# Loading parts of wo and W2 as two and six runs in an interleaved attention and MLP decode kernel

## The chip, the cores and the metric

The kernel runs on one core of one Trainium2 chip. A core has five engines that run their own instruction streams: TensorE (PE, with its weight loads PEld), VectorE (DVE), ScalarE (ACT), GpSimd (POOL) and SyncE (SP). Sixteen DMA engines move data between HBM and SBUF, the core's memory, which has 128 partitions (rows). Transfers are issued here by SP and by ACT, each with a queue of its own (q1 and q10 in the profile). The metric is device time in microseconds (us), the median over runs.

## The reference

One token passes four blocks: attention with a cached K and V, an MLP, and both again with the same weights and caches.

```python
def _A_ref(x, k_cache, v_cache, wq, wo):          # B=1, Sq=1, D=640, H=32, Sk=8192, Dh=128
    q = (x @ wq).reshape(B, Sq, H, Dh).transpose(0, 2, 1, 3)
    scores = jnp.einsum("bhqd,bhkd->bhqk", q, k_cache) * (Dh ** -0.5)
    p = _softmax(scores, axis=-1)
    o = jnp.einsum("bhqk,bhkd->bhqd", p, v_cache)
    return o.transpose(0, 2, 1, 3).reshape(B, Sq, H * Dh) @ wo

def _B_ref(x, w1, w2):                            # w1 [640, 1728], w2 [1728, 640]
    h = jnp.einsum("bsd,df->bsf", x, w1)
    return jnp.einsum("bsf,fd->bsd", jnp.maximum(h, 0), w2)

x = A_x
x = x + _A_ref(_layernorm(x), K, V, wq, wo)
x = x + _B_ref(_layernorm(x), w1, w2)
x = x + _A_ref(_layernorm(x), K, V, wq, wo)
x = x + _B_ref(_layernorm(x), w1, w2)
```

All data are float32. K and V together are 268 MB and are read twice, but for a few pieces that are kept.

## The kernel before

**Two layers.** `attention_and_mlp(L, ...)` runs for L = 0 (called layer 1 here) over heads 0 to 31 and for L = 1 (layer 2) over heads 31 to 0. Each head has a K unit and a V unit of 4 MB (128 partitions by 8,192 floats), loaded whole or, for a few heads, in pieces.

**The ring.** Units live in one SBUF tile, `ring`. `pump()` issues loads on SP's queue in a fixed order, and each as soon as a free place is found; in the bulk of layer 1 the ring has room for three whole units. `release()` frees a piece after TensorE's last use of it and calls `pump()`. So the load that takes the place of head 6's V unit is issued when the last V piece of head 6 has been multiplied.

**One head.** `scores` (line 433) multiplies the four pieces of K, VectorE takes the maximum (445, 451), ScalarE the exponentials (459), VectorE transposes them (466), `values` (484) multiplies the four pieces of V, and `output` (501 to 525) collects the result. All streams are in order: what stands behind a waiting instruction on its engine waits too.

**Side work.** Between the pieces, `side_work()` takes steps from two lists, `chores` and `slow`. `slow` holds the next group's queries and, at fixed heads, the preparation of the last head's projection. For that, `due()` at the fifth head after the first of layer 1 (`WC_AT[0] = 5`) issues on ACT's queue a load of one block of wo, 128 rows of 2,560 B, into the tile `mix` (line 676). One head later the generator `mixing()` joins `slow`: VectorE sums the rows (543) and subtracts the mean (544), TensorE transposes the block (550, 556), ScalarE copies it out (552, 564). Later `mixing_quarter()` multiplies it with W1 (571). Layer 2 does the same at head position 8.

**The MLP.** `mlp()` multiplies the hidden row with W2's 14 blocks (`times_rows`, line 402, called in `product`). Blocks 0 to 7 are in `w2_t`. In layer 2 blocks 8 to 13 go into a free place of the ring (`w2_rest`): `pump()` issues them last, by `W2_MORE` as blocks 8 and 9, 10 and 11, 12, and 13 (line 173). Block 13 has 64 rows (`W2_LAST`), the others 128. Their products are the last of the kernel, and behind them stand one VectorE instruction (858) and the output's transfer (901).

**Layout.** `_laid_out` (line 922) puts the inputs on the host into the order in which they are loaded; it does no arithmetic.

Of the kernel before, what the change touches and what calls it, by code (L numbers as in the profile page):

```python
# [15 lines left out]
P = 128  # L16
D = 640
H = 32
SK = 8192
DH = 128  # L20
# [3 lines left out]
HG = 4  # L24
NG = H // HG
# [41 lines left out]
def wide(kind, piece):  # L67

    return 4 * piece[2] * (1 if kind == "k" else DH) // 8


def size(unit):
    return sum(wide(unit[0], piece) for piece in unit[1])
# [6 lines left out]
FB = 4 * F_TILES + F_REST  # L80
SLOTS = 8
W2_PARTS = [(0, 4), (4, SLOTS)]
W2_MORE = [(SLOTS, 10), (10, 12), (12, 13), (13, FB)]
W2_LAST = 2 * (F_ROWS[2] - P * F_TILES)


@with_exitstack
def decode_kernel(ctx: ExitStack, tc: tile.TileContext, x, kv, wq, wo, w1, w2, out):
    nc = tc.nc
    consts = ctx.enter_context(tc.tile_pool(name="consts", bufs=1))  # L90
    wts = ctx.enter_context(tc.tile_pool(name="wts", bufs=1))
# [25 lines left out]
    w2_rest = []  # L117
# [8 lines left out]
    def place(layer, u, n):  # L126


        step = 8 if u in KEPT else max(m for m in (8, 64, 256, 512) if n % m == 0)
        low, high = 0, RING if layer else FLAT  # L130
        if layer == 0 and u in kept and (u in KEPT or u[0] == 30 and UNITS[30][u[1]][0] == "k"):
            low, high = (EDGE, RING) if u in KEPT else (FLAT, EDGE)
        at, best = low, None
        for a, m in sorted(live.values()) + [(high, 0)]:
            a = min(a, high)
            if a - at >= n and (best is None or a - at < best[1]):
                best = at, a - at
            at = max(at, -(-(a + m) // step) * step)
        return None if best is None else best[0]

    def pump():
        while todo:
            layer, u = todo[0]
            kind, pieces = unit = UNITS[u[0]][u[1]]
            n = size(unit)
            at = place(layer, u, n)
            if at is None:
                return
            todo.pop(0)
            o = dram_at[u]  # L150
            nc.sync.dma_start(
                ring[:, 8 * at : 8 * (at + n)],
                kv[o : o + 8 * P * n].rearrange("(p m) -> p m", p=P),
            )
            for t, piece in enumerate(pieces):
                m = wide(kind, piece)
                live[layer, u, t] = at, m
                at_of[layer, u, t] = ring, 8 * at
                at += m
            if not todo or layer < todo[0][0]:  # L160
                for a, b in W2_PARTS[:: 1 - 2 * layer]:
                    nc.sync.dma_start(w2_t[:, a:b], w2[:, a:b])
        n = (FB - SLOTS) * D // 8
        if not w2_rest:
            at = place(1, None, n)
            if at is not None:
                w2_rest.append(ring[:, 8 * at : 8 * (at + n)].rearrange("p (b d) -> p b d", d=D))
                for a, b in W2_MORE:
                    more_of_w2(a, b, w2_rest[0][:, a - SLOTS : b - SLOTS])

    def more_of_w2(a, b, where):
        rows = W2_LAST if a == FB - 1 else P
        nc.sync.dma_start(where[:rows], w2[:rows, a:b])
# [68 lines left out]
    mix = consts.tile([P, DFF], F32, name="mix")  # L242
# [55 lines left out]
    def spread_of_columns(xc):  # L298
        sq = work.tile([P, NB], F32, name="ln_sq")
        ss = work.tile([P, 1], F32, name="ln_ss")  # L300
        nc.vector.scalar_tensor_tensor(
            sq, xc, 1.0, xc, op0=ALU.mult, op1=ALU.mult, accum_out=ss
        )
        pv = bank_tile()[:, :1]
        nc.tensor.matmul(pv, ss.to_broadcast([P, P]), ones, start=True, stop=True)
        return inv_std(pv)
# [286 lines left out]
    def attention_and_mlp(L, xr, s, before=None):  # L593

        heads = list(range(H))[:: 1 - 2 * L]
        last = heads[-1]
# [60 lines left out]
        def due(h):  # L657

            where = heads.index(h)
            k, j = divmod(where, HG)  # L660
            if j == 0:
                o_cols[k] = work.tile([P, HG], F32, name="o_cols", bufs=2)
            if where and j == 0:
                chores.append([run_out(k - 1), "pe"])
            if j == 2 and k + 1 < NG:
                slow.append([queries_of(k + 1), "pe"])
            if where == H - 2:
                chores.append([first_of_last(), "pe"])
            if where == H - 1:
                chores.append([before_last(), "pe"])  # L670
            if L == 0 and where == H - HG:
                slow.append([centre_query(NG - 1, HG - 1), "pe"])
            if L == 0 and where == 4:
                nc.scalar.dma_start(w1_t, w1)
            if where == WC_AT[L]:
                nc.scalar.dma_start(mix[:, :D], wo[last // HG][:, last % HG])
            if where == WC_AT[L] + 1:
                slow.append([mixing(), "dve"])
            if where in MIX_AT[L]:
                slow.append([mixing_quarter(MIX_AT[L].index(where)), "pe"])  # L680
# [28 lines left out]
        for where, h in enumerate(heads):  # L709
# [21 lines left out]
            if h == last:  # L731
                o = work.tile([P, 1], F32, name="c_ol")
                rest = output(hd, o)
# [15 lines left out]
            else:  # L749
                k, j = divmod(where, HG)  # L750
# [8 lines left out]
    def mlp(L, o, last, xp, ph):  # L759
# [162 lines left out]
def _laid_out(A_x, A_k_cache, A_v_cache, A_wq, A_wo, B_w1, B_w2):  # L922
    k = np.asarray(A_k_cache)[0].reshape(H, 4, 4, RUN, DH).transpose(0, 4, 1, 2, 3)
    v = np.asarray(A_v_cache)[0].reshape(H, 4, 4, NBL, 4, 32, DH).transpose(0, 1, 5, 3, 4, 2, 6)
    v = v.reshape(H, P, NBL, 4, 4, DH)
    kv = np.empty(H * P * SK * 2, k.dtype)
    o = 0
    for h in range(H):
        for kind, pieces in UNITS[h]:
            n = 8 * sum(wide(kind, piece) for piece in pieces)  # L930
            block = kv[o : o + P * n].reshape(P, n)
            o += P * n
            a = 0
            for piece in pieces:
                if kind == "k":
                    r, c, m = piece
                    part = k[h, :, :, r, c : c + m]
                else:
                    b, r, m = piece
                    part = v[h, :, b, :, r : r + m]  # L940
                part = part.reshape(P, -1)
                block[:, a : a + part.shape[1]] = part
                a += part.shape[1]
    w2 = np.zeros((P, FB, D), np.asarray(B_w2).dtype)
    for b, f in enumerate(_hidden_rows()):
        w2[f >= 0, b] = np.asarray(B_w2)[f[f >= 0]][:, _COLS]

    wq = np.asarray(A_wq).reshape(NB, P, NG, HG * DH).transpose(2, 1, 0, 3)
    return {
        "x": np.repeat(np.asarray(A_x).reshape(D)[_COLS].reshape(4, DR), 32, axis=0),  # L950
        "kv": kv,
        "wq": wq.reshape(NG * P, NB * HG * DH),
        "wo": np.asarray(A_wo)[:, _COLS].reshape(NG, HG, DH, D).transpose(0, 2, 1, 3),
        "w1": np.asarray(B_w1).reshape(NB, P, DFF).transpose(1, 0, 2),
        "w2": w2,
    }


# [22 lines left out]
```

## Time and profile before

| | us |
|---|---|
| median of 3 runs | 1353.76 (1351.77 to 1354.28) |
| the profiled execution | 1351.81 |
| its span, first to last instruction | 1349.9 |
| PE, DVE, ACT busy in it | 909.9, 297.2, 58.5 |

The page tells the bulk; the windows tell how busy the 16 DMA engines are in a stretch (the share in the last but one column, where 1.00 is all sixteen); the timeline tells one instruction's start, its duration and, in brackets, the idle time of its engine before it and what ended that. A DMA's landing is told as the time from its issue until the data are there.

```profile
q1 hardware_dynamic: 24936, 530.95, 91.9%
q10 hardware_dynamic: 4608, 41.86, 7.4%
```

These are SP's and ACT's queues: packets, MB, and the share of the sixteen engines' span that they took.

### The profile page before, as it was taken

The numbers are of one execution on the slowest core, as the hardware profiler recorded it, in microseconds if no ns is written. First come the engines' busy times: TensorE is split into PE (matmuls) and PEld (weight loads), VectorE is DVE, ScalarE is ACT, GpSimd is POOL, SyncE is SP. The second block draws the span as 40 slices with busy tenths as digits, with TensorE's granted clock in tenths as the row PEclk, the third lists the DMA queues.
The fourth block names the chain that finished last, engine by engine and source line by source line (L and its number), as shares of the span: only waits on it lengthen the run. The fifth ranks groups of instructions, "written<-read, shape, count | busy, mean of one in ns | idle before, by whom it ended". The sixth has DMA issues, their size and how long they took to land.

```text
span 1349.9 us, 14049 instructions
## 1 busy us (share of the span) xinstructions
PE 909.9 (67%) x6078; PEld 282.3 (21%) x6078; DVE 297.2 (22%) x979; ACT 58.5 (4%) x147; POOL 2.9 (0%) x10
## 2 busy tenths in 40 slices
PE   5564676766667666666688776677566767668667
PEld 2111121211112112112143211222112221122113
DVE  2121121222112222122223222221121212212212
ACT  0000000000000000000000000000000000000000
POOL 0000000000000000000000000000000000000000
PEclk8676788788777777777998876778778787787889
DMA  9999999999999999999999999999999999999997
GB/s 396 435 429 430 431 429 432 432 429 432 431 429 429 430 432 430 433 425 421 428 373 426 435 430 430 429 431 431 429 432 432 425 436 428 429 434 428 432 425 325
DMA packets 29605, 573.71 MB, mean 425 GB/s; under 512 B 3300, under 2 KB 3432, under 8 KB 6376
## 3 DMA queue, kind: packets, MB, share of 16 engines
q1 hardware_dynamic: 24936, 530.95, 91.9%
q10 hardware_dynamic: 4608, 41.86, 7.4%
q8 instruction: 48, 0.79, 0.2%
q14 instruction: 13, 0.11, 0.0%
HBM read 572.80 MB, written 0.00 MB: 424 GB/s over the span
## 4 chain that ended last, share of the span: by engine, by line
DMA 70%; PE 26%; DVE 2%; issue 1%; ACT 1%; SPq 0%; ACTq 0%; DVEq 0%
DMA ring<-in_kv 69%; PE outs L484 9%; PE ps L433 9%; PE px L571 2%; PE px L360 2%; DMA ring<-in_w 1%; PE acc L402 1%; PE pm L471 1%; PE px L374 1%; ACT p L459 0%; DVE h_t L445 0%; PE pm L450 0%; PE px L402 0%; DVE p L505 0%; DVE p L466 0%
## 5 line engine op out<-in xcount | busy, mean ns | idle before, releaser
L484 PE MATMUL outs<-ring,p 128*4 128x512 f32 (+2 forms) x2160 | 347.7, 773 | 162.4 <-DMA ring<-in_kv 109.7
L433 PE MATMUL ps<-ring,spread_q 128*32 128x512 f32 (+2 forms) x2056 | 334.0, 746 | 122.6 <-DMA ring<-in_kv 121.9
L445 DVE TENSOR_REDUCE h_t<-ps 128x1 f32<-128x512 f32 x64 | 44.3, 691 | 389.4 <-PE ps L433 389.3
L433 PEld LDWEIGHTS ps<-ring,spread_q 128*32 128x32 f32 x2056 | 71.6, 130 | 261.0 <-issue 229.1
L484 PEld LDWEIGHTS outs<-ring,p 128*4 128x4 f32 x2160 | 51.4, 96 | 325.5 <-issue 162.6
L459 ACT ACTIVATE p<-ps,h_t 128x512 f32<-128x512 f32 x63 | 43.3, 687 | 1179.0 <-DVE h_t L451 1179.0
L466 DVE STREAM_TRANSPOSE p<-p 128x128 f32<-128x128 f32 x256 | 79.8, 312 | 63.6 <-ACT p L459 56.9
L518 PE MATMUL pm<-ones,p 128*128 128x1 f32 (+1 forms) x128 | 24.7, 263 | 97.6 <-DVE p L505 97.6
L501 DVE TENSOR_SCALAR p<-outs,ind 128x128 f32<-128x128 f32 x64 | 22.5, 351 | 251.5 <-PE outs L484 251.5
L505 DVE SCALAR_TENSOR_TENSOR p<-outs,ind,p 128x128 f32<-128x128 f32 x188 | 66.0, 351 | 6.7
L450 PE MATMUL pm<-ident,h_t 128*128 128x128 f32 x128 | 31.2, 325 | 40.5 <-DVE h_t L445 40.4
L518 PEld LDWEIGHTS pm<-ones,p 128*128 128x128 f32 x128 | 19.2, 190 | 161.1 <-DVE p L505 160.3
L471 PEld LDWEIGHTS pm<-ind,h_t 128*128 128x128 f32 x128 | 27.4, 266 | 82.6 <-issue 82.6
L372 DVE TENSOR_SCALAR q_row<-px,ln_r 128x128 f32<-128x128 f32 x56 | 19.5, 349 | 109.1 <-PE ps L433 71.4
L571 PE MATMUL px<-w_t,wct 128*128 128x448 f32 (+1 forms) x80 | 43.4, 627 | 0.0
L360 PE MATMUL px<-wq_t,ln_xc 128*32 128x512 f32 x140 | 41.4, 921 | 0.0
L474 DVE RECIPROCAL h_t<-pm 128x1 f32<-128x1 f32 x64 | 10.7, 168 | 119.4 <-PE pm L471 119.4
L450 PEld LDWEIGHTS pm<-ident,h_t 128*128 128x128 f32 x128 | 19.0, 187 | 85.5 <-DVE h_t L445 83.8
L471 PE MATMUL pm<-ind,h_t 128*128 128x1 f32 x128 | 32.9, 326 | 0.0
L402 PE MATMUL acc<-wo_t,o_cols 128*32 128x160 f32 x496 | 31.1, 408 | 0.0
L402 PEld LDWEIGHTS acc<-wo_t,o_cols 128*32 128x32 f32 x496 | 24.3, 151 | 17.6 <-issue 14.2
L374 PEld LDWEIGHTS px<-sel,q_row 128*128 128x128 f32 x112 | 19.9, 221 | 35.1 <-DVE q_row L372 35.1
(126 smaller groups left out, 227.3 us busy)
## 6 DMA issues: line engine op xcount, KB each, us to landing
ring<-in_kv SPq DMA_DIRECT2D x104, 4096.0 KB, 28.8
ring<-in_kv SPq DMA_DIRECT2D x29, 2048.0 KB, 27.9
wq_t<-in_wq ACTq DMA_DIRECT2D x14, 1280.0 KB, 16.7
wo_t<-in_wo ACTq DMA_DIRECT2D x14, 1280.0 KB, 17.2
ring<-in_kv SPq DMA_DIRECT2D x9, 1024.0 KB, 14.9
w_t<-in_w SPq DMA_DIRECT2D x4, 1280.0 KB, 26.8
w_t<-in_w ACTq DMA_DIRECT2D x1, 4320.0 KB, 24.4
ring<-in_kv SPq DMA_DIRECT2D x5, 768.0 KB, 19.4
```

The lines of the kernel that those rows point to most:

```text
L360: nc.tensor.matmul(pq[32 * strip : 32 * strip + 32], xc[:, c : c + 1].to_broadcast([P, 32]), wq_t[g][:, c], start=c < 4, stop=c in (1, 2, ...
L402: nc.tensor.matmul(acc[32 * g : 32 * g + 32, :DR], col.to_broadcast([col.shape[0], 32]), wt[:, g * DR : (g + 1) * DR], start=first, stop=last,
L433: nc.tensor.matmul(hd.ps[32 * g : 32 * g + 32, c : c + n], spread_q[:, 3 - r : 35 - r], tile_of[:, at + g * n : at + (g + 1) * n], start=f ...
L445: nc.vector.tensor_reduce(hd.nm, hd.ps, AX.X, ALU.max, negate=True)
L450: nc.tensor.matmul(pt[:, :P], hd.nm.to_broadcast([P, P]), ident, start=True, stop=True)
L459: nc.scalar.activation(hd.p, hd.ps, AF.Exp, bias=hd.low, scale=scale, accum_out=hd.l)
L466: nc.vector.transpose(hd.all_p[:, b * P : (b + 1) * P], hd.p[:, b * P : (b + 1) * P])
L471: nc.tensor.matmul(pt[:, :1], hd.l.to_broadcast([P, P]), ind[:, 4:5], start=True, stop=True)
L484: nc.tensor.matmul((hd.out if r0 < 2 else hd.out_2)[32 * g : 32 * g + 4, r0:r1].rearrange("p r d -> p (r d)"), hd.all_p[:, 32 * i : 32 * i ...
L505: nc.vector.scalar_tensor_tensor(oc, hd.out[:, r], ind[:, r : r + 1], oc, op0=ALU.mult, op1=ALU.add)
L518: nc.tensor.matmul(pt[:, :n], part, mask.to_broadcast([P, n]), start=i == 0, stop=i == len(parts) - 1,)
L571: nc.tensor.matmul(pt[:, :n], wct[:, c], w1_t[:, c, f : f + n], start=(c == 0), stop=(c == NB - 1),)
```

## The change

A new input `apart` holds copies of three pieces of weights, each cut into runs of whole rows with a gap of 128 floats (`GAP`) after each run. A load from it has the shape runs x rows x 640 on the side of HBM, and rows x 640 in SBUF; the gap keeps the runs from being one.

- Layer 1, wo's block into `mix`: rows 80 to 127 are loaded from `wo` as before, rows 0 to 79 from `apart` as two runs of 40.
- Layer 2, W2's block 12: rows 0 to 79 from `w2`, rows 80 to 127 from `apart` as six runs of 8.
- Layer 2, W2's block 13: its 64 rows from `apart` as two runs of 32.

Layer 1's loads of W2 and layer 2's load of wo stay. What is computed stays too.

```diff
+GAP = 128
+FEW = {"wo": (0, 80, 2), "w2": (80, P, 6), "w2_last": (0, W2_LAST, 2)}
+def few_size(name):
+    r0, r1, k = FEW[name]
+    return (r1 - r0) * D + k * GAP
...
-                for a, b in W2_MORE:
-                    more_of_w2(a, b, w2_rest[0][:, a - SLOTS : b - SLOTS])
+                rest = w2_rest[0]
+                for a, b in W2_MORE[:2]:
+                    more_of_w2(a, b, rest[:, a - SLOTS : b - SLOTS])
+                whole = FEW["w2"][0]
+                nc.sync.dma_start(rest[:whole, FB - SLOTS - 2], w2[:whole, FB - 2])
+                by_few_engines(nc.sync, "w2", rest[:, FB - SLOTS - 2])
+                by_few_engines(nc.sync, "w2_last", rest[:, FB - SLOTS - 1])
+
+    def by_few_engines(queue, name, where):
+
+        r0, r1, k = FEW[name]
+        at, n = FEW_AT[name], few_size(name)
+        part = apart[at : at + n].rearrange("(k m) -> k m", k=k)
+        queue.dma_start(
+            where[r0:r1], part[:, : n // k - GAP].rearrange("k (r d) -> k r d", d=D)
+        )
...
             if where == WC_AT[L]:
-                nc.scalar.dma_start(mix[:, :D], wo[last // HG][:, last % HG])
+                whole = 0 if L else FEW["wo"][1]
+                nc.scalar.dma_start(mix[whole:, :D], wo[last // HG][whole:, last % HG])
+                if L == 0:
+                    by_few_engines(nc.scalar, "wo", mix[:, :D])
```

In `_laid_out` the pieces are copied into `apart`. The order of the instructions on TensorE and VectorE is the same; two DMA queues have one issue more each. On ACT's queue in layer 1, around heads 4 to 6, it stood before as (line, operation, destination and source, shape):

```order
L213 DMA wo_t<-in_wo 128x2560
L459 ACTIVATE p,h_t<-ps,h_t 128x512
L676 DMA mix<-in_wo 128x640
L459 ACTIVATE p,h_t<-ps,h_t 128x512 x2
L209 DMA wq_t<-in_wq 128x2560
L552 COPY wct<-px 128x512
```

and now, with the changed kernel's line numbers:

```order
L237 DMA wo_t<-in_wo 128x2560
L483 ACTIVATE p,h_t<-ps,h_t 128x512
L701 DMA mix<-in_wo 48x640
L191 DMA mix<-in_apart 80x1x640
L483 ACTIVATE p,h_t<-ps,h_t 128x512 x2
L233 DMA wq_t<-in_wq 128x2560
L576 COPY wct<-px 128x512
```

One load became two in the same place. On SP's queue at the end of the program it stood before as:

```order
L162 DMA w_t<-in_w 128x2560 x2
L173 DMA ring<-in_w 128x1280 x2
L173 DMA ring<-in_w 128x640
L173 DMA ring<-in_w 64x640
L901 DMA out<-xr 4x160
```

and now:

```order
L172 DMA w_t<-in_w 128x2560 x2
L197 DMA ring<-in_w 128x1280 x2
L182 DMA ring<-in_w 80x640
L191 DMA ring<-in_apart 48x1x640
L191 DMA ring<-in_apart 64x1x640
L928 DMA out<-xr 4x160
```

Two loads became three. The instructions that read `mix` first stand on TensorE, in head 6 of layer 1, as they stood before (changed kernel's lines; 574 is the transposing of the block, 508 `values`):

```order
L508 MATMUL outs_113<-ring,p 4x512 x4
L495 MATMUL pm<-ind,h_t 128x1
L398 MATMUL px<-sel,q_row 128x1
L508 MATMUL outs_113<-ring,p 4x512 x8
L574 MATMUL px<-ident,mix 128x128 x4
L508 MATMUL outs_113<-ring,p 4x512 x4
```

Nothing moved here: the block's transposes stand between the third and the fourth piece of head 6's V.

More of the change, by code (lines that the diff above doesn't have):

```diff
@@ L84, with decode_kernel @@
 W2_LAST = 2 * (F_ROWS[2] - P * F_TILES)
+GAP = 128
[3 more added lines that the diff above has]
+    return (r1 - r0) * D + k * GAP
+FEW_AT = {name: sum(few_size(n) for n in list(FEW)[:i]) for i, name in enumerate(FEW)}
 @with_exitstack
-def decode_kernel(ctx: ExitStack, tc: tile.TileContext, x, kv, wq, wo, w1, w2, out):
+def decode_kernel(ctx: ExitStack, tc: tile.TileContext, x, kv, wq, wo, w1, w2, apart, out):
     nc = tc.nc
@@ L946, in _laid_out @@
         w2[f >= 0, b] = np.asarray(B_w2)[f[f >= 0]][:, _COLS]
+    wo = np.asarray(A_wo)[:, _COLS].reshape(NG, HG, DH, D).transpose(0, 2, 1, 3)
+    apart = np.zeros(sum(few_size(name) for name in FEW), w2.dtype)
+    for name, block in (("wo", wo[-1][:, -1]), ("w2", w2[:, FB - 2]), ("w2_last", w2[:, FB - 1])):
+        (r0, r1, m), at, n = FEW[name], FEW_AT[name], few_size(name)
+        part = apart[at : at + n].reshape(m, -1)
+        part[:, : n // m - GAP] = block[r0:r1].reshape(m, -1)
     wq = np.asarray(A_wq).reshape(NB, P, NG, HG * DH).transpose(2, 1, 0, 3)
@@ L952, in _laid_out @@
         "wq": wq.reshape(NG * P, NB * HG * DH),
-        "wo": np.asarray(A_wo)[:, _COLS].reshape(NG, HG, DH, D).transpose(0, 2, 1, 3),
+        "wo": wo,
         "w1": np.asarray(B_w1).reshape(NB, P, DFF).transpose(1, 0, 2),
         "w2": w2,
+        "apart": apart,
     }
```

## The prediction

> **What bounds the kernel now.** I read the page first: the slices, the queues, the chain of waits.
>
> ```profile
> DMA  9999999999999999999999999999999999999997
> DMA packets 29605, 573.71 MB, mean 425 GB/s; under 512 B 3300, under 2 KB 3432, under 8 KB 6376
> q8 instruction: 48, 0.79, 0.2%
> DMA 70%; PE 26%; DVE 2%; issue 1%; ACT 1%; SPq 0%; ACTq 0%; DVEq 0%
> ```
>
> The transfers bound it: the 16 DMA engines are busy in every slice but the last, and 70% of the chain is waiting for them. 425 GB/s over 16 engines is 26.6 GB/s each, so one row of 2,560 B occupies an engine for 0.1 us, one row of a whole ring load (32,768 B) for 1.23 us, and a whole load (4,096 KB) all sixteen for 9.87 us. Time is lost only where engines stand idle, or where one of them has more to do than the rest. So the next view is the busy share of the engines in the last microseconds (the last but one column).
>
> ```profile
> 1338.00:1339.00 1.00, 0.96 (x14) 0.45 (x6) 0.59 (x3) 0.08 (x1) 0.00 (x0) 1.00 1.09 446
> 1340.00:1341.00 1.00, 1.00 (x32) 0.82 (x29) 0.05 (x1) 0.00 (x0) 0.00 (x0) 1.00 0.69 271
> 1341.00:1342.00 1.00, 1.00 (x26) 0.85 (x22) 0.32 (x3) 0.00 (x0) 0.00 (x0) 1.00 0.59 241
> 1342.00:1343.00 1.00, 1.00 (x32) 0.73 (x24) 0.69 (x4) 0.00 (x0) 0.00 (x0) 1.00 0.57 236
> 1343.00:1344.00 1.00, 1.00 (x22) 0.71 (x18) 0.16 (x1) 0.00 (x0) 0.27 (x1) 1.00 0.55 220
> 1344.00:1345.00 1.00, 0.61 (x20) 0.42 (x16) 0.00 (x0) 0.00 (x0) 0.28 (x1) 1.00 0.39 137
> ```
>
> A share of 0.56 is nine engines of sixteen. Seven have emptied their queues by about 1341, nine work on until 1344 to 1345.5, though each was given the same bytes: seven are 4 to 5 us ahead. At the layers' boundary it is the same, with 0.56 to 0.58:
>
> ```profile
> 691.00:692.00 1.00, 1.00 (x20) 0.56 (x16) 0.00 (x0) 0.00 (x0) 0.00 (x0) 1.00 0.96 406
> 693.00:694.00 1.00, 0.70 (x6) 0.70 (x6) 0.18 (x1) 0.25 (x1) 0.00 (x0) 1.00 0.56 236
> 694.00:695.00 1.00, 0.69 (x10) 0.32 (x13) 0.22 (x1) 0.00 (x0) 0.00 (x0) 1.00 0.58 246
> ```
>
> The chain says who waits for the nine:
>
> ```profile
> 1330.05 15.50 DMA ring<-in_w
> 1345.59 0.93 PE px L402 x16
> ```
>
> **The change, part by part: the tail.** W2's block 12 now comes as 80 rows over all engines (5 each), 48 rows in six runs, and block 13's 64 rows in two runs. No row shows whether a load of k runs occupies just k engines; I take it so for the sum, and the other end is a rival below. Then each of ten engines loses 3 rows of block 12 and 4 of block 13, or 7 x 0.1 = 0.7 us; two engines carry 5 + 8 + 32 = 45 rows in place of 12, 3.3 us more; four carry 13 in place of 12. If the two are among the seven early ones, they end near 1340 + 3.3, still ahead of the nine, and the end comes 0.7 us sooner. If one is among the nine, it ends 3.3 us after some moment between 1344.3 and 1345.5, some 2.6 us past the present end. No row names the engines; I keep both ends and take their middle, +1.0.
>
> [...]
>
> **The wo block.** 48 rows now go over all engines (3 each), then 80 rows in two runs: 40 on each of two engines, which carry 43 rows in place of 8. In bytes that is 3.5 us on two engines and 0.5 us less on the rest. What counts is when the last row lands, since VectorE waits for it. How a load on ACT's queue shares an engine with the ring's loads on SP's queue is read from the landings.
>
> ```profile
> wo_t<-in_wo ACTq DMA_DIRECT2D x14, 1280.0 KB, 17.2
> DMA to landing us min/median/max: 15.9/19.6/23.3
> mix<-in_w SPq DMA_DIRECT2D x1, 640.0 KB, 4.8
> ```
>
> The second line is the wo block (320 KB, 8 rows an engine; line 676). It takes at least 15.9 us, while 640 KB on SP's queue at the boundary, beside a nearly empty ring queue, takes 4.8; and wo_t with four times its bytes takes hardly more (17.2). So it isn't bytes that cost but rows: each waits for one ring row. 8 x (1.23 + 0.1) = 10.6 us, and for wo_t's rows (10,240 B, 0.39 us) 8 x 1.62 = 13.0; both leave 4 to 5 us for starting. A row's turn is 1.33 us. Now the place where it is needed:
>
> ```profile
> 123.80 0.33 ACTq L676 DMA_DIRECT2D mix<-in_wo  x1
> 171.83 0.81 DVE L543 TENSOR_REDUCE m_s<-mix 128x1 f32<-128x640 f32 x1
> 172.67 0.82 DVE L544 SCALAR_TENSOR_TENSOR mix<-m_s,mix 128x640 f32<-128x640 f32 x1
> 175.17 1.11 PE L550 MATMUL px<-ident,mix 128*128 128x128 f32 x4
> 176.21 1.32 PE L484 MATMUL outs<-ring,p 128*4 128x512 f32 x8
> 177.60 0.33 SPq L151 DMA_DIRECT2D ring<-in_kv  x1
> 179.89 1.64 PE L433 MATMUL ps<-ring,spread_q 128*32 128x512 f32 x8 [0.33 <-DMA ring<-in_kv]
> 187.63 0.33 SPq L151 DMA_DIRECT2D ring<-in_kv  x1
> 190.85 1.04 PE L484 MATMUL outs<-ring,p 128*4 128x512 f32 x8 [1.98 <-DVE p L466]
> 196.87 0.33 SPq L151 DMA_DIRECT2D ring<-in_kv  x1
> 200.47 1.74 PE L433 MATMUL ps<-ring,spread_q 128*32 128x512 f32 x8 [1.64 <-DMA ring<-in_kv]
> ```
>
> Before, the block landed at 123.8 + 23.3 = 147.1 and was read at 171.83, 24.7 us later. Now 35 more turns of 1.33 us put the last row at 193.7. One thing cuts that short: when the ring's queue on the two engines runs dry, rows no longer wait. The load issued at 177.60 landed by 200.4, so its bytes began about 200.4 - 9.87 = 190.5; the ones before it, plus 3.5 us of extra rows, are through by 191.5 (an engine 2 us ahead) to 194. I take 192.5, a stall of 20.7 us for L543.
>
> What stands behind it: on VectorE the whole of head 6's output; on TensorE L550, which stands ahead of the last V piece of head 6. L550 starts when L544 is done, at 192.5 + 1.7 + 0.1 = 194.3 in place of 175.17, so the piece ends, and its ring place is free, 19.2 us later: SP issues at 196.8 in place of 177.60. The ring queue has run dry at 190.5. From issue to landing that load now needs 9.87 us and a start of between 0.33 us (the issue alone) and 3.3 us (the 4.8 us above, less 640 KB at full rate, 1.5): it lands at 207.0 to 210.0 instead of 200.4. That is 6.6 to 9.6 us of idle transfer engines, and I take 7.5, near the short end, since in the row of 4.8 us some engines still had other work. It isn't paid again on the next loads: their issues follow at 187.63 - 177.60 = 10.0 and 196.87 - 187.63 = 9.2 us (0.33 of the first is a wait for DMA), no slower than a load passes. Nor is it won back: transfers bound the layer, and at the boundary (share 0.56 and idle) everything after follows TensorE. The idle stretch lets the late engines catch up, so the 0.5 us saved by the rest is worth nothing there.
>
> The added issues (one on ACT, one on SP) cost 0.33 us each.
>
> ```profile
> L459 ACT ACTIVATE p<-ps,h_t 128x512 f32<-128x512 f32 x63 | 43.3, 687 | 1179.0 <-DVE h_t L451 1179.0
> ring<-in_w SPq DMA_DIRECT2D x1, 160.0 KB, 13.3
> ```
>
> The one on ACT stands ahead of exponentials that wait 1179.0 / 63 = 18.7 us each for VectorE, the one on SP ahead of nothing but the output, 13.3 us before its data land. Both are hidden. Should SP's show, it is 0.3 us.
>
> **The sum.** 7.5 + 1.0 = +8.5 us, against the profiled execution's own 1351.81 us (span 1349.9): 1360.3. The median of the runs shown, 1353.76, stands 1.95 above that execution; on it the forecast is 1362.3.
>
> **The rivals.**
>
> *No stall, so not slower.* The place is the two engines' choice between the queues. If they took several small rows for one ring row, the 40 would be in early. The point that decides: the rows start at about 147.1 - 10.6 = 136.5, so 43 must pass by 171.83, in under 0.82 us each. Then wo costs nothing and gives 0.5 us at the boundary, the tail 0.7: 1353.76 - 1.2 = 1352.6. Against it: 15.9 us for 8 rows. For it: only that no run of 40 stands in this trace. [...] 0.17.
>
> *The loads aren't confined.* If the two and six runs are spread over all sixteen engines after all, nothing moves but two issues: 1353.8. For it: no row shows a confined load. 0.05.
>
> *A shorter stall.* If both engines are far ahead, or the other queue gets more than its turn once the ring thins, the rows are in by 188, SP issues at 192.3, and the idle is 3 us: with the tail's 0.7 gained, 1356.1. 0.12.
>
> *Both engines among the nine late ones.* The rows end at 194 or later, the start is the long one, 9.6, and the tail loses 2.6: 1366. 0.14.
>
> **How the numbers follow.** The forecast has 0.52, and its own range is 1359.7 to 1366.0 (1353.76 + 6.6 - 0.7 to 1353.76 + 9.6 + 2.6). For 8 in 10 I go from 1352.4, which takes in the rival without a stall, to 1367. A measurement of this kernel can tell about 0.2%, 2.7 us, from no change. Slower by more: forecast, shorter stall (its 2.3 us are just below the bound, so part of it counts as within) and late engines, 0.52 + 0.12 + 0.14 = 0.78, of which 0.03 goes to within. Within 0.2%: the unconfined loads, most of the rival without a stall and that part, 0.05 + 0.11 + 0.03 = 0.19. Faster: the remaining 0.06, for a gain larger than worked out.
>
> **What would show it.** In the changed profile L543 stands at 190 to 194 with a wait for the DMA of some 18 to 21 us before it; L550 and the ring issue after head 6 follow 19 us late; a stretch near 190 to 198 has a DMA share far below 1; the load with two runs lands 60 us or more after its issue. At the end, the share falls to 0.56 about 0.7 us sooner and to 2 of 16 (0.13) only if the two engines come last. I am wrong in the main step if L543 still starts near 172, and wrong about the ring if it is late but the DMA share there stays at 1.

## The result and the profile after

| | before | after |
|---|---|---|
| median, us | 1354.02 (1351.77 to 1354.94, 4 runs) | 1363.83 (1362.7 to 1366.82, 4 runs) |
| profiled execution, us | 1351.81 | 1362.7 |
| its span, us | 1349.9 | 1360.9 |

The ratio is 1.0081 with an interval of 1.0068 to 1.0094: the change costs 9.2 to 12.7 us. The forecast was 1362.3.

The engines do the same work. What changed is the transfers. From the page of the changed kernel, the busy tenths of the DMA engines, their GB/s in 40 slices of 34 us, and the chain of waits:

```profile
DMA  9999989999999999999999999999999999999997
GB/s 394 431 437 430 406 343 418 430 432 433 428 431 429 428 435 428 430 431 420 427 380 419 432 435 428 430 429 429 434 430 430 427 434 430 432 427 431 431 426 308
DMA 71%; PE 24%; DVE 2%; another core or an unknown queue 1%; issue 1%; ACT 0%; ACTq 0%; SPq 0%; DVEq 0%
```

Against the page before, one slice stands out: the sixth (170 to 204 us) has 343 GB/s, where it had 429, and an 8 where 9s were. The one before it has 406 instead of 431, with a 9. (The dip in the twenty-first, 380, was there before, with 373: it is the boundary of the layers.) So there are two different losses next to each other: in one the engines are idle, in the other they are busy and move less. The timeline of the changed kernel shows what stands there (line numbers have moved: 567 was 543, 574 was 550, 508 was 484, 161 was 151). The first column is the start, the second the duration, the bracket the idle time before and what ended it:

```profile
125.67 0.34 ACTq L701 DMA_DIRECT2D mix<-in_wo  x1
126.06 1.21 ACTq L191 DMA_DIRECT2D mix<-in_apart  x1
191.07 0.82 DVE L567 TENSOR_REDUCE m_s<-mix 128x1 f32<-128x640 f32 x1 [17.60 <-DMA mix<-in_apart]
191.93 0.83 DVE L568 SCALAR_TENSOR_TENSOR mix<-m_s,mix 128x640 f32<-128x640 f32 x1
192.85 1.09 PE L574 MATMUL px<-ident,mix 128*128 128x128 f32 x4 [16.06 <-DVE mix L568]
193.87 1.89 PE L508 MATMUL outs<-ring,p 128*4 128x512 f32 x8
195.82 0.33 SPq L161 DMA_DIRECT2D ring<-in_kv  x1
```

The two-run load is issued at 126.06, and VectorE's sum of the rows (567) waits 17.60 us for it, until 191.07: 65 us from issue to use. TensorE's transpose (574) waits 16.06 us for VectorE, head 6's last V piece (508) stands behind it, and SP's next ring load, which was issued at 177.60 before, follows at 195.82. The windows of the changed kernel give the price (the last three columns are the granted clock, the DMA share and GB/s):

```profile
130.00:190.00 60.00, 27.99 (x158) 7.73 (x150) 9.66 (x31) 1.56 (x4) 0.00 (x0) 0.75 1.00 411
190.00:210.00 20.00, 13.91 (x74) 4.44 (x74) 5.74 (x15) 1.63 (x4) 0.00 (x0) 0.73 0.71 282
190.00:195.00 5.00, 2.15 (x12) 0.83 (x12) 1.65 (x2) 0.59 (x1) 0.00 (x0) 0.50 0.17 73
195.00:200.00 5.00, 3.37 (x22) 1.26 (x22) 1.62 (x5) 0.00 (x0) 0.00 (x0) 0.50 0.70 256
```

The same two long stretches of the kernel before:

```profile
130.00:190.00 60.00, 42.02 (x232) 11.87 (x224) 13.80 (x40) 3.11 (x8) 0.00 (x0) 0.78 1.01 432
190.00:210.00 20.00, 13.24 (x106) 4.73 (x106) 4.65 (x15) 1.38 (x4) 0.00 (x0) 0.91 1.00 427
```

In 190 to 210 the share falls to 0.71, and (427 - 282) / 427 x 20 = 6.8 us of transfers are missing: the stall. By the share alone the engines are idle for (1.00 - 0.71) x 20 = 5.8 us of it. In 130 to 190 the share is 1.00 as before, yet the same busy engines move 411 GB/s instead of 432: (432 - 411) / 432 x 60 = 2.9 us are missing without any idle time. Together 9.7 us.

A window counts a transfer with all its bytes where it starts, so short windows scatter: undisturbed, the kernel before reads 419 to 447 GB/s in the windows of 10 us from 110 to 250. The trace also keeps a record of each row that an engine moved, with its start, duration and size, and these don't scatter: from 130 to 190 a ring row (32,768 B) takes 1.217 us in the mean before and 1.268 after. So the slowing is real, 4%. How much of it remains is read from a product that stands at each layer's end (its weight load; the last two numbers are its first start, in layer 1, and its last, in layer 2). Before:

```profile
L584 PEld LDWEIGHTS acc<-mix,c_ol x16: 105/106/108, 694.5 to 1337.4; 128*32 128x32 f32 x16
```

After:

```profile
L608 PEld LDWEIGHTS acc<-mix,c_ol x16: 105/106/108, 703.7 to 1347.5; 128*32 128x32 f32 x16
```

It is 9.2 us late in layer 1 and 10.1 in layer 2, and the span ends 11.0 us late, so the tail itself has 0.9 in this execution. Its windows and, from the timeline, its last products on TensorE, in the changed kernel:

```profile
1350.00:1351.00 1.00, 1.00 (x32) 0.88 (x32) 0.12 (x1) 0.00 (x0) 0.00 (x0) 1.00 0.71 179
1351.00:1352.00 1.00, 0.98 (x22) 0.70 (x18) 0.26 (x3) 0.00 (x0) 0.00 (x0) 1.00 0.67 253
1352.00:1353.00 1.00, 1.00 (x32) 0.87 (x32) 0.75 (x4) 0.00 (x0) 0.00 (x0) 1.00 0.72 274
1353.00:1354.00 1.00, 0.83 (x18) 0.58 (x14) 0.16 (x1) 0.00 (x0) 0.12 (x1) 1.00 0.66 159
1354.00:1355.00 1.00, 0.47 (x16) 0.14 (x5) 0.00 (x0) 0.00 (x0) 0.43 (x1) 1.00 0.52 121
```

```profile
1356.39 1.43 PE L426 MATMUL px<-ring,hT 128*32 128x160 f32 x32 [1.92 <-DMA ring<-in_w]
```

Here too a busy engine moves less than before, for a part of the time: at a share of 0.71 it is 179 / (16 x 0.71) = 15.8 GB/s for each, and 15.1 at 0.66, where the prediction's row at 0.69 had 271 / (16 x 0.69) = 24.5. In the two microseconds between, at 0.67 and 0.72, it is 23.6 and 23.8, nearly as before. The records agree: a row of 5,120 B takes 0.312 us in the mean from 1350 to 1351 and 0.331 from 1353 to 1354, 0.211 and 0.210 between, and 0.196 to 0.206 before from 1340 to 1343. TensorE waits 1.92 us for the last blocks.

### The profile page after: what moved, and what is told of

It reads as the page before. It is cut to its first block, busy times and chain, and to the rows that moved or that the text cites. A ratio compares the mean times of both kernels' runs of the same rounds, so it can differ in the third digit from the quotient of the medians.

```text
span 1360.9 us, 14054 instructions
## 1 busy us (share of the span) xinstructions
PE 914.1 (67%) x6078; PEld 283.3 (21%) x6078; DVE 297.3 (22%) x979; ACT 58.5 (4%) x147; POOL 2.9 (0%) x10
## 4 chain that ended last, share of the span: by engine, by line
DMA 71%; PE 24%; DVE 2%; another core or an unknown queue 1%; issue 1%; ACT 0%; ACTq 0%; SPq 0%; DVEq 0%
DMA ring<-in_kv 67%; PE ps L457 10%; PE outs L508 7%; PE px L384 2%; DMA w_t<-in_w 2%; PE px L595 2%; DMA ring<-in_w 2%; PE acc L426 1%; DMA wq_t<-in_wq 1%; PE px L398 1%; PE pm L495 1%; DVE p L529 0%; DVE h_t L469 0%; ACT p L483 0%
## 5 line engine op out<-in xcount | busy, mean ns | idle before, releaser
L508 PE MATMUL outs<-ring,p 128*4 128x512 f32 (+2 forms) x2160 | 351.7, 782 | 158.3 <-DMA ring<-in_kv 106.3
L398 PEld LDWEIGHTS px<-sel,q_row 128*128 128x128 f32 x112 | 19.9, 221 | 34.9 <-DVE q_row L396 34.9
```

The lines of the kernel that those rows point to most:

```text
L508: nc.tensor.matmul((hd.out if r0 < 2 else hd.out_2)[32 * g : 32 * g + 4, r0:r1].rearrange("p r d -> p (r d)"), hd.all_p[:, 32 * i : 32 * i ...
```

## The experiments

Theory 1 is the prediction's: the last row lands late, VectorE's wait keeps a ring place from coming free, and the ring's queue runs dry. Theory 2: the load itself costs time, wait or no wait, by what it does to the transfers beside it. Theory 3: it is not the few engines that make the load late but its form (a source in three dimensions, with a gap). Ratios are against the kernel before.

**Each half alone.** First the tail's part, with wo loaded as before; then the wo part, with W2 loaded as before.

```diff
# the tail alone, against the changed kernel
-                whole = 0 if L else FEW["wo"][1]
-                nc.scalar.dma_start(mix[whole:, :D], wo[last // HG][whole:, last % HG])
-                if L == 0:
-                    by_few_engines(nc.scalar, "wo", mix[:, :D])
+                nc.scalar.dma_start(mix[:, :D], wo[last // HG][:, last % HG])
# wo alone, against the changed kernel
-                for a, b in W2_MORE[:2]:
+                for a, b in W2_MORE:
...
-                whole = FEW["w2"][0]
-                nc.sync.dma_start(rest[:whole, FB - SLOTS - 2], w2[:whole, FB - 2])
-                by_few_engines(nc.sync, "w2", rest[:, FB - SLOTS - 2])
-                by_few_engines(nc.sync, "w2_last", rest[:, FB - SLOTS - 1])
```

> wo's block is loaded whole as before; W2's blocks 12 and 13 keep their six and two runs. Theory 1 (the wait: VectorE waits for the last wo row, and the ring runs dry meanwhile): the wait at the summing of wo's block is 0, and about 9 of the 9.8 us go. What is left is the tail: -0.7 us if the two engines that carry 45 rows are among the seven early ones (1353.3), +2.6 if one is among the nine late ones (1356.6). Theory 2 (imbalance: every load waits for the engine with most bytes, so the two engines' extra bytes are paid wherever they stand): 3.3 us for the tail's 33 extra rows, 1357.3. Theory 3 (the form of the load is dear in itself): two of its three loads are left, so about two thirds, 1360.

> W2's last blocks are loaded as before; only wo's block keeps its two runs. Theory 1: the wait stays 17 to 18 us and the DMA share in 190 to 195 us stays below 0.3, so the whole loss but the tail's part: 1354.0 + 9.2 = 1363.2. Theory 2: 3.5 us for 35 extra rows on two engines, 1357.5. Theory 3: one load of three, 1357.3.

Measured: the tail alone 1353.74 us, ratio 1.001 (1.0002 to 1.0019), 1.4 us over the kernel before, with an interval of 0.3 to 2.6; wo alone 1362.3, ratio 1.0074 (1.006 to 1.0088), 10.0 us over it. The two parts add up, and nearly all of the loss is wo's. Windows of the tail alone:

```profile
1339.00:1340.00 1.00, 1.00 (x18) 0.46 (x6) 0.50 (x2) 0.00 (x0) 0.00 (x0) 1.00 0.95 266
1340.00:1341.00 1.00, 0.91 (x11) 0.77 (x10) 0.50 (x5) 0.37 (x2) 0.00 (x0) 1.00 0.86 246
1345.00:1346.00 1.00, 0.17 (x8) 0.00 (x0) 0.00 (x0) 0.00 (x0) 0.37 (x1) 1.00 0.59 142
1346.00:1347.00 1.00, 0.00 (x0) 0.00 (x0) 0.00 (x0) 0.00 (x0) 0.00 (x0) 1.00 0.20 46
```

The share is still 0.59 up to 1346, not down to 0.13 as it would if two engines alone came last, and already at a share of 0.95 the rate is 266 GB/s. The engines are busy longer with the same bytes; they aren't waiting for two stragglers.

**The same load, without the wait.** The wo load is issued three heads earlier, so that its last row lands well before it is read.

```diff
-            if where == WC_AT[L]:
+            if where == (WC_AT[L] if L else 2):
```

> The changed kernel, but layer 1's wo block (48 rows whole, 80 rows in two runs) is issued at the third head instead of the sixth, some 60 us sooner, with the same bytes on the same engines. Theory 1: the rows are in long before 172 us, no wait at the summing, the DMA share stays at 1 around 190 us; the time is that of before less what the late engines save, 1.2 us: 1352.8 (1353.3 to 1356.6 if the tail's two engines are late). Theory 2: the bytes stay, so the loss stays, 3.5 us at least, 1357.5 or more. Theory 3: nothing changes, 1363.8.

Measured: 1355.89, ratio 1.0022 (1.0014 to 1.0031), 3.0 us over the kernel before by the ratio. VectorE's sum starts without a wait, which would stand in brackets:

```profile
175.91 0.82 DVE L567 TENSOR_REDUCE m_s<-mix 128x1 f32<-128x640 f32 x1
```

So the wait accounts for (1.0081 - 1.0022) x 1354 = 8.0 us of the loss, and theory 1 holds for that part. At the layers' boundary, without the tail, it is much the same: the product that stands at 694.5 before and at 703.7 in the changed kernel is at 696.4 here, 7.3 us earlier. Of the rest the tail explains 1.4; 1.6 us stay with the wo load although nothing waits for it. The windows in which the load is now in progress:

```profile
60.00:70.00 10.00, 5.72 (x25) 1.44 (x26) 0.35 (x1) 0.00 (x0) 0.00 (x0) 0.50 1.02 412
70.00:80.00 10.00, 7.90 (x46) 2.80 (x48) 3.60 (x12) 0.78 (x2) 0.00 (x0) 0.84 0.98 396
80.00:90.00 10.00, 7.31 (x42) 1.86 (x38) 1.62 (x5) 0.00 (x0) 0.00 (x0) 0.67 1.00 413
```

The same windows of the tail alone, where wo is loaded later and as before:

```profile
60.00:70.00 10.00, 6.87 (x36) 1.75 (x36) 0.70 (x2) 0.00 (x0) 0.00 (x0) 0.66 1.00 428
70.00:80.00 10.00, 7.90 (x46) 2.64 (x46) 3.24 (x11) 0.78 (x2) 0.00 (x0) 0.71 0.96 413
80.00:90.00 10.00, 7.39 (x46) 1.75 (x38) 1.75 (x6) 0.00 (x0) 0.00 (x0) 0.78 1.04 446
```

Full share and 412, 396, 413 GB/s instead of 428, 413, 446: 66 GB/s less over 10 us, 1.5 us of transfers in these three windows. The records agree, with 1.284 us for a ring row from 60 to 90 where the tail alone has 1.218. The two windows before, from 40 to 60, lack 33 GB/s more, so the slowing is 2.3 us in these five; at the boundary 1.9 us are left of it (696.4 against 694.5). Theory 2 holds for this part.

**A shorter wait.** 64 rows go to the two runs instead of 80, 32 for each instead of 40.

```diff
-FEW = {"wo": (0, 80, 2), "w2": (80, P, 6), "w2_last": (0, W2_LAST, 2)}
+FEW = {"wo": (0, 64, 2), "w2": (80, P, 6), "w2_last": (0, W2_LAST, 2)}
```

> The changed kernel, but 64 of wo's rows in two runs instead of 80: 32 + 4 rows on each of the two engines instead of 40 + 3. Theory 1: 7 turns of 1.3 us less, so the last row lands 9 us sooner, near 182, and the wait at the summing is 8 to 9 us instead of 17.6. The ring has about 10 us in store at that place (the load that is issued at 177.6 starts moving at 188 to 190), so a wait of 8 to 9 us costs 0 to 1 us: 1354 to 1356. The loss falls off a step, not in proportion. Were it in proportion to the wait, half of 9.2 would be left, 1358.5. Theory 2: in proportion to the extra rows, 28 of 35, so 80% of it is left. Theory 3: 1363.8.

Measured: 1354.7, ratio 1.0016 (1.0007 to 1.0024), 2.2 us over by the ratio. From the timeline, and then from the windows of this kernel:

```profile
180.64 0.82 DVE L567 TENSOR_REDUCE m_s<-mix 128x1 f32<-128x640 f32 x1 [7.88 <-DMA mix<-in_apart]
185.38 0.33 SPq L161 DMA_DIRECT2D ring<-in_kv  x1
```

```profile
185.00:190.00 5.00, 3.37 (x32) 1.23 (x28) 1.62 (x5) 0.27 (x1) 0.00 (x0) 0.90 0.99 425
190.00:195.00 5.00, 4.60 (x23) 1.21 (x22) 0.98 (x2) 0.00 (x0) 0.00 (x0) 1.00 1.01 434
```

The last row lands 191.07 - 180.64 = 10.4 us earlier. Not all of that is due to the rows: ACT issued this load at 122.89, 3.2 us sooner than at 126.06, and in the records the first small row goes out at 134.3 instead of 136.6, 2.3 us sooner. The other 8.1 us are for 7 rows fewer on each of the two engines (32 + 4 in place of 40 + 3), 1.2 us a row, a little below the prediction's turn of 1.33 us. And VectorE waits 7.88 us, SP's issue is 7.8 us late, and the transfers don't notice: a share of 0.99 and 1.01. The ring has that much in store. In the changed kernel SP's issue was 195.82 - 177.60 = 18.2 us late, and 5.8 (idle) to 6.8 us (missing) of transfers were lost; so the store is worth 11 to 12 us, and the wait costs only what goes beyond it. What is left of the 2.2 us beside the tail's 1.4 fits the slowing: in the records a ring row takes 1.256 us from 130 to 190, and at the boundary the product stands at 695.7, 1.2 us late.

**Sixteen runs.** If the form of the load made it late (theory 3), sixteen runs of five rows would be late too.

```diff
-FEW = {"wo": (0, 80, 2), "w2": (80, P, 6), "w2_last": (0, W2_LAST, 2)}
+FEW = {"wo": (0, 80, 16), "w2": (80, P, 6), "w2_last": (0, W2_LAST, 2)}
```

> The changed kernel with one number different: layer 1's 80 rows of wo are loaded as sixteen runs of five rows instead of two runs of forty. Same issue on ACT's queue, same place, same bytes, same rows, same gap between runs; W2's tail as in the change. Theory 1 (two runs are served by two DMA engines, so the last row lands late and VectorE waits): sixteen runs spread over all engines, the load is done within some 10 us of the others, VectorE's reduction of wo starts without a wait of more than 2 us, SP's issues to the ring are as before, and what is left over the kernel before is the tail's part alone, 1354 (1353 to 1355). Rival 3 (a load with three dimensions in its source, or with a gap, is slow whatever its runs): wait at the reduction of 15 us or more and 1362 again. Theory 2 (two confined engines slow the other engines' packets): bytes per second in the stretch 140 to 180 us return to those of the kernel before.

Measured: 1355.43, ratio 1.0016 (1.0007 to 1.0025). The sum starts without a wait:

```profile
173.85 0.82 DVE L567 TENSOR_REDUCE m_s<-mix 128x1 f32<-128x640 f32 x1
```

So theory 3 falls: with the same form it is the small number of runs that makes the load late. But it was not 1354, the tail's part alone, and the rate did not return to that of before:

```profile
130.00:140.00 10.00, 3.98 (x30) 1.10 (x26) 1.62 (x5) 0.00 (x0) 0.00 (x0) 0.84 1.03 404
140.00:150.00 10.00, 6.18 (x37) 1.60 (x32) 2.23 (x6) 0.78 (x2) 0.00 (x0) 0.67 1.02 412
```

The kernel before in these two windows:

```profile
130.00:140.00 10.00, 5.07 (x30) 1.20 (x26) 1.62 (x5) 0.00 (x0) 0.00 (x0) 0.67 1.04 447
140.00:150.00 10.00, 5.85 (x38) 1.38 (x30) 2.23 (x6) 0.78 (x2) 0.00 (x0) 0.84 1.01 433
```

64 GB/s less over 10 us is 1.5 us, with sixteen runs in the load; in the records a ring row takes 1.307 us from 130 to 150, and 1.215 before. So the slowing isn't a matter of two runs, and theory 2 had to be taken apart.

**Probes.** To the kernel before, six loads were added that are not part of the computation: 64 rows of 2,544 B each, as two runs with a gap, from kv into a part of W2's tile that is loaded later anyway. The three kernels differ only in the partitions that the rows go to.

```diff
+ROW = 636
+PROBE_AT = (8, 11, 14, 17, 20, 23)
...
+            if L == 0 and where in PROBE_AT:
+                runs = kv[: 2 * (32 * ROW + 128)].rearrange("(k m) -> k m", k=2)
+                nc.scalar.dma_start(
+                    w2_t[:64, 0, :ROW], runs[:, : 32 * ROW].rearrange("k (r d) -> k r d", d=ROW)
+                )
# on 8 partitions: w2_t[:8, :, :ROW]; from partition 64 on: w2_t[64:72, :, :ROW]
```

> The kernel before with six more loads that are not part of the computation: 64 rows of 2,544 bytes each, as two runs of 32 rows with a gap, from kv into a part of W2's tile that nothing uses until layer 2, on ACT's queue after heads 8, 11, 14, 17, 20 and 23 of layer 1, one row on each of 64 partitions. Nothing waits for them except W2's load much later. 1 MB more in all against some 430 GB/s is 2.3 us if all engines shared it; confined to two engines it is some 19 us more on each of two. Theory 2a (a confined load slows the other engines because its rows lie on partitions that those serve): GB/s at full share falls by 3% or more while a probe is in progress, and more than in p2 and p3; time 1358 or more. Theory 2b (only the bytes count, and the imbalance of two engines is made up): all three probes alike, 1354 to 1357. Theory 2c (two engines behind hold up the ring as in the change): all alike and 1365 or more.

> As the probe on 64 partitions, same source, bytes, rows, runs and places in the program, but the 64 rows of each load go to partitions 0 to 7, eight on each. Theory 2a (foreign partitions): less slowing than on 64 partitions if the confined engines serve these partitions anyway, nearer to 1354. Theory 2b and 2c: the same as on 64 partitions.

> As the probe on partitions 0 to 7, but on partitions 64 to 71. Theory 2a: slowing between, by which engines serve these partitions. Theory 2b and 2c: the same as the other two.

Measured: 1370.95 on partitions 0 to 63, ratio 1.013 (1.0117 to 1.0144); 1368.08 on 0 to 7, 1.0107 (1.0093 to 1.0121); 1372.39 on 64 to 71, 1.0139 (1.0125 to 1.0153); the kernel before 1352.51. By the medians all three lose 15.6 to 19.9 us (14.5 to 18.8 by the ratios) for 1 MB that is worth 2.3 us, though nothing waits for the rows. 32 rows of 2,544 B at 26.6 GB/s would be 0.0956 x 32 = 3.06 us of an engine's time, six times 18.4. By this estimate the loss is about what the two engines have to do in addition (theory 2c), a little less in the fastest of the three. The windows of the probe on 64 partitions show how:

```profile
420.00:430.00 10.00, 7.08 (x30) 2.03 (x30) 1.69 (x6) 0.00 (x0) 0.00 (x0) 0.66 0.96 394
430.00:440.00 10.00, 7.90 (x48) 2.65 (x52) 3.60 (x12) 0.78 (x2) 0.00 (x0) 0.80 0.88 359
```

The share falls below 1, to 0.88. I read it so, though no view names the engines: two are behind with their part of the ring's loads, a piece isn't complete without them, its place doesn't come free, and the other engines run out of work. It shows only after several probes; while the first is in progress, from 200 to 240, the share is full:

```profile
200.00:240.00 40.00, 26.95 (x182) 7.67 (x182) 7.84 (x26) 2.09 (x5) 0.00 (x0) 0.87 1.01 425
```

On partitions 0 to 7:

```profile
200.00:240.00 40.00, 27.38 (x182) 7.78 (x182) 7.96 (x26) 2.09 (x5) 0.00 (x0) 0.83 1.01 431
```

On partitions 64 to 71:

```profile
200.00:240.00 40.00, 27.03 (x178) 7.77 (x182) 7.84 (x25) 2.09 (x5) 0.00 (x0) 0.83 1.01 419
```

The kernel before:

```profile
200.00:240.00 40.00, 28.16 (x180) 8.13 (x180) 6.56 (x21) 2.09 (x5) 0.00 (x0) 0.83 1.01 431
```

So there is a second, smaller loss that depends on where the rows go (theory 2a): none on partitions 0 to 7, 1.4% on 0 to 63, 2.8% on 64 to 71, in the order of the three times. The records have the same order, with 1.218, 1.244 and 1.259 us for a ring row, and 1.219 before.

**Which partitions, and whether the form matters.** Theory A is a guess about which engine serves which partitions, which no view shows and the expectations take as given: if the engines divided a load's rows in order, each would have eight partitions of its own in the ring's loads of 128 rows, the division would fall elsewhere in a load of 80, 64 or 48 rows, and an engine that writes to partitions that another one is serving would slow both. Theory B: gaps and three dimensions are slow in themselves. Two versions of the wo load and two probes tell them apart:

```diff
# 128 rows in sixteen runs, against the changed kernel
-FEW = {"wo": (0, 80, 2), "w2": (80, P, 6), "w2_last": (0, W2_LAST, 2)}
+FEW = {"wo": (0, P, 16), "w2": (80, P, 6), "w2_last": (0, W2_LAST, 2)}
# and mix[whole:] isn't loaded in layer 1
# two plain loads of 80 and 48 rows, against the changed kernel
-                    by_few_engines(nc.scalar, "wo", mix[:, :D])
+                    nc.scalar.dma_start(mix[:whole, :D], wo[last // HG][:whole, last % HG])
# probe of 64 plain rows, six times, against the kernel before
+                rows = kv[: 64 * D].rearrange("(r d) -> r d", d=D)[:, :ROW]
+                nc.scalar.dma_start(w2_t[:64, 0, :ROW], rows)
# probe of 128 plain rows, three times (heads 8, 14, 20)
+                rows = kv[: P * D].rearrange("(r d) -> r d", d=D)[:, :ROW]
+                nc.scalar.dma_start(w2_t[:, 0, :ROW], rows)
```

> The changed kernel, but all 128 rows of wo in layer 1 are loaded as sixteen runs of eight rows with a gap between, and the contiguous load of 48 rows is left out; W2's tail as in the change. The load in sixteen runs of five rows lowered the bytes per second to 404 and 412 in 130 to 150 us, at full share, against 447 and 433 before, and left the kernel 2.9 us above the kernel before. Theory A (an engine that writes rows to partitions that another engine serves in the ring's loads slows the others): sixteen runs of eight rows put each engine on its own eight partitions as a 128-row load does, so bytes per second in that stretch stay within 2% of before, and the time is that of the tail alone, 1353.7. Theory B (the gapped source or its three dimensions slow the load): the dip stays, 1355.4.

> The changed kernel, but layer 1's first 80 rows of wo come from wo itself, rows with the stride that the kernel before has, as a second load beside that of the 48 rows: no runs, no gap, only two loads instead of one. W2's tail as in the change. Theory A: 80 rows are five to each of sixteen engines, which puts all but the first on partitions that another engine serves, so the dip in 130 to 150 us is there (415 or less against 440 before) and the time is 1355.4. Theory B: no dip, 1353.7.

> The kernel before with six loads that are not part of the computation, of 64 rows of 2,544 bytes to partitions 0 to 63 at the places of the two-run probes (heads 8 to 23 of layer 1), but as rows of one stride from kv, no runs: four rows for each of sixteen engines instead of 32 for each of two. The bytes alone are worth 2.3 us over six loads. Theory C (what a load on few engines costs is those engines' own time, 3.0 us for 32 rows, six times, added in full once the store is used up): without the two engines it goes to 1354.8 by the bytes alone; with theory A's slowing of 1 to 1.5 us for each load on foreign partitions, 1361 to 1364. If it stays near 1371, the confinement was not the cost of the two-run probes.

> As the last probe with the same bytes, as three loads of 128 rows of 2,544 bytes to all 128 partitions after heads 8, 14 and 20, eight rows for each of sixteen engines, on the partitions that it serves in the ring's loads. Theory A: no slowing beyond the bytes, 1354.8 (1354 to 1356), and clearly below the probe on partitions 0 to 63. If foreign partitions do not matter, both are alike.

Measured, against 1352.62: 128 rows in sixteen runs 1355.98, ratio 1.0023 (1.0014 to 1.0032); two plain loads 1356.09, 1.002 (1.0011 to 1.0028); 64 plain rows six times 1360.43, 1.006 (1.0047 to 1.0074); 128 plain rows three times 1355.18, 1.002 (1.001 to 1.0029). First the two probes, which carry the same bytes. 64 rows, while the first is in progress:

```profile
200.00:210.00 10.00, 5.53 (x68) 2.57 (x68) 2.76 (x8) 0.78 (x2) 0.00 (x0) 0.96 1.04 390
```

128 rows:

```profile
200.00:210.00 10.00, 5.53 (x68) 2.57 (x68) 2.80 (x8) 0.78 (x2) 0.00 (x0) 0.96 1.05 447
```

390 against 447 GB/s at the same share (428 in the kernel before, and 447 is within the scatter); from 200 to 210 a ring row takes 1.389 us in the first and 1.217 in the second. The times differ by 5.3 us, though I had expected 6 or more. The bytes themselves, three loads of 128 rows, cost 2.6 us against the 2.3 worked out. As plain rows the 64-row probe is 10.5 us below its two-run form on the same partitions, although it slows the transfers more while it lasts (390 GB/s here): most of the two-run probe's loss came with the two runs. Now the two plain loads, of 80 and 48 rows:

```profile
130.00:140.00 10.00, 3.34 (x26) 0.89 (x22) 1.62 (x5) 0.00 (x0) 0.00 (x0) 0.67 1.02 409
140.00:150.00 10.00, 5.29 (x30) 1.45 (x22) 2.23 (x6) 0.78 (x2) 0.00 (x0) 0.67 1.01 381
```

No gap, no runs, no third dimension, and the dip is deeper than with sixteen runs of five: theory B falls as an explanation of these. But the sixteen runs of eight rows, which by theory A are like a load of 128, have the dip too:

```profile
130.00:140.00 10.00, 4.77 (x30) 1.06 (x25) 1.62 (x5) 0.00 (x0) 0.00 (x0) 0.67 1.03 411
140.00:150.00 10.00, 4.89 (x34) 1.38 (x30) 2.23 (x6) 0.78 (x2) 0.00 (x0) 0.84 1.01 396
```

411 and 396 against 447 and 433; in the records a ring row takes 1.315 us from 130 to 150. Theory A expected no dip there, and that was wrong. Either its guess about the partitions is wrong too, or it isn't the cause.

The records name neither the engine nor the partition of a transfer. But where the share is full, sixteen are in progress at a time (in the kernel before from 130 to 190; seventeen or eighteen in 7% of the samples, where one's end overlaps the next one's start), and each begins within 20 ns of the end of another. Strung together they make sixteen chains, which I take for the sixteen engines. With the probe on partitions 64 to 71, from 285 to 295 us, two chains carry the probe's rows, by turns with ring rows of 1.255 and 1.256 us in the mean. Two other chains, which carry none of them, have ring rows of 1.340 and 1.344; the remaining twelve have 1.252 to 1.256. With the probe on partitions 0 to 7 (280 to 290) all sixteen have 1.215 to 1.217. So the two that are slowed most have no part in the load. Whether they serve these eight partitions, as theory A would need, isn't shown, nor why the others lose 3% as well, so the cause stays open. What the runs show is narrower: rows beside the ring's loads slowed the ring's transfers in every form tried but two, the plain 128 rows (1.217 us for a ring row) and the rows on partitions 0 to 7 (1.218, with 1.219 before).

None of these kernels was faster than the kernel before.

## Why the prediction was right, and where it was not

**The load on few engines is late: right.** I had taken it without a row that showed it. In the records from 142.3 us on the 80 small rows lie on two chains, 40 on each, and on each a small row and an entry of the ring's queue take turns; the last row starts at 190.1. With sixteen runs the wait is gone. So the rival in which the loads aren't confined is out, and so is the one in which an engine takes several small rows for one ring row: it needed under 0.82 us a row, and what the records show is one small row and then one entry of the other queue, from the first of the 40 rows to the last, 47.8 us for the 39 steps of the chain that ends last.

**The chain from the wait to the ring: right in each link.** The wait was to be 18 to 21 us and was 17.60, just short of it; the transpose at 194.3 came at 192.85, the ring issue at 196.8 came at 195.82, the share, far below 1 in the forecast for 190 to 198, is 0.17 from 190 to 195 and 0.70 from 195 to 200. The early issue without the wait gives 8.0 us back (7.3 at the boundary); that is the shown cause of most of the loss.

**The size of the stall: 7.5 predicted, right as a landing, too much as idle time.** The prediction took the lateness of the next ring load's landing for idle time. In the records that load ends at 207.6, inside the predicted 207.0 to 210.0 and 7.6 us later than before (200.0). In the windows of 190 to 210 6.8 us of transfers are missing, but by the share the engines are idle for only 5.8 us, below the bound of 6.6; the rest of the 6.8 is engines that are busy and move less. VectorE's wait ended 1.4 us before the 192.5 that I took. One reason is in the records: between the 40 rows of the chain that ends last, 35 steps are 1.31 to 1.42 us long (1.35 in the mean), but four are 0.1 us, where the ring's entry was one of 4 bytes, which takes 0.009 us. I had counted each step as a ring row's turn.

**What the sum left out.** The layer-1 term as a whole is 9.2 us at the layers' boundary, not 7.5, because the load slowed the transfers beside it, 2.9 us by the windows of 130 to 190 (4% by the records). The step that failed is the price of the rows in bytes: I counted 0.1 us of their own engine for each and nothing for the others. It cost the forecast little: 1363.83 against 1362.3.

**The tail: the number right by luck.** I took +1.0 as the middle between two early engines (-0.7) and one late (+2.6). No run shows the rows that this sum gives to each engine. The tail alone measured +1.4 (0.3 to 2.6). But the share neither falls sooner nor ends in two engines; those that are still busy move less for a part of the time. Neither end of my range for this term describes that. That the confined engines were early ones would fit the wo load as well, which, issued early, cost 1.6 us and no more, with 3.5 us of extra rows on two engines; no view names them.

**Smaller steps.** ACT's issue of the two-run load took 1.21 us, not 0.33 (of the sixteen-run loads 0.62 and 0.67). The transfers stayed at a full share behind it (1.00 from 130 to 190), so it was hidden all the same. That the stall isn't won back was right: 9.2 us late in layer 1, 10.1 in layer 2. That the 0.5 us saved by the other engines is worth nothing was not tested.

## What to carry to other kernels

When a load is put on few engines beside a busy queue, price it by turns: rows on its most loaded engine times the time of one row of the other queue (here 40 rows in 48 us, 1.2 us a row), and compare the landing with the moment of use plus what the ring holds in store (here 11 to 12 us); a wait of 7.88 us inside that store left no engine idle, one of 17.60 us left the transfers idle for the rest. With all engines busy, more work for two of them delayed the end here: one load, early enough, cost 1.6 us in all, and six cost 15.6 to 19.9 us, about the 18.4 us estimated for the two engines' own time. And look at GB/s beside the share: a full share at a lower rate is a loss that no wait shows.

## What was not expected of the hardware

- Small loads slowed the large ones beside them at a full DMA share: a ring row takes 1.389 us beside the probe of 64 plain rows and 1.217 beside that of 128, and 1.218, 1.244 or 1.259 us by the partitions that the rows of a two-run load go to. With the rows on partitions 64 to 71 two chains that carry none of them are slowed most (1.34 us). Why is not settled.
- The rate of a busy engine isn't fixed in the tail either: 15.8 GB/s for each at a share of 0.71 after, 23.6 a microsecond later, and 24.5 at 0.69 before (0.312, 0.211 and 0.206 us for a row of 5,120 B).
- The issue of a load in two runs takes ACT 1.21 us, that of one in sixteen runs 0.62 or 0.67, that of the plain rows beside them 0.34.
